# Chunk attention and two MoE layers on one core: exponentials head by head with the maximum as bias, and another order of the first loads

## The chip, the cores and the metric

The kernel runs on one core of a Trainium2 chip. Five engines work side by side, each through its own queue in program order: TensorE (PE, matrix products, with the weight loads listed as PEld), VectorE (DVE), ScalarE (ACT), GpSimd (POOL) and SyncE (SP, which here issues the DMA transfers). The metric is the device time of one execution in microseconds (us); lower is better. Time before the change: 1680.23 us, the median of three runs (1678.89 to 1683.86).

## What is computed

```python
scores = scale * np.matmul(q_c, k_c.transpose(0, 1, 2, 4, 3))   # chunks of 64 tokens, 8 heads, 64 wide
scores = scores - np.max(scores, axis=-1, keepdims=True)
attn = np.exp(scores)
attn = attn / (np.sum(attn, axis=-1, keepdims=True) + 1e-09)
x = np.matmul(attn, v_c)                                        # laid out as 4608 tokens x 512
h = x @ w_in1                                                   # 512 -> 2048
x = (np.maximum(h, 0) + alpha * np.minimum(h, 0)) @ w_out1      # 2048 -> 512
h = x @ w_in2
out = (h - np.tanh(h)) @ w_out2
```

The weights and alpha arrive as 64-bit numbers and are turned into 32-bit ones on the chip; q, k and v are 32-bit.

## The kernel before

The 4608 tokens are cut into 36 tiles of 128 and into 9 blocks of 512 (four tiles). Every float32 product of the two layers is made from three products of rounded halves ("hi" and "lo"), which the code calls `split`. The program is written out by hand in its final order: what stands first in the source stands first in the queue of its engine.

**The opening** handles tiles 0 to 3 and ends when block 0 can be multiplied. For each tile: `att_a_early` transposes q and k on PE (into `tr`) and copies the result out (`qt`, `kt`, line 290 on DVE or 292 on ACT); `att_s_early` makes the scores with 32 small matmuls (line 335); `att_e` takes the maximum of each head over the 64 scores (`mx`, DVE, line 348), subtracts it (`p`, DVE, line 350) and takes the exponential of all eight heads in one instruction (ACT, line 353); `att_n` sums (DVE, line 359), adds 1e-9 (361), takes the reciprocal (362) and multiplies (363, on POOL for tiles 0 to 2); `att_t_early` transposes `p` on PE (`ptr`, line 403) and copies it out on ACT (405); `att_v_early` multiplies by v (418); `att_x` splits the result into xh (ACT, 435) and xl (DVE, 439). The scores of tiles 0 to 3 go in turn to the two halves of one tile `first_banks`, two PSUM banks that are called `first` in the trace.

**Weights.** The first piece is "s0", the second "s1", then pairs 0, 1, 2 and so on. `load_w` issues the transfer, `convert_a` makes two ACT passes (lines 113 and 116, or 113 and 162), `convert_b` four DVE passes that the code numbers as ops 0 to 3 (lines 126, 130, 132, 136), and `split_w` a rounded copy on ACT (174) and a difference (181). The buffer `wr` that `convert_low` (162) writes exists once, so it waits for op 3 of the piece before.

**The step loop.** A step multiplies one block by one of the 16 column pieces of w_in1 (`up`, line 455, 12 matmuls), applies the activation (`act_g`, lines 467 to 469) and, two steps later, multiplies by w_out1 (`down`, line 511). Steps 0 to 7 run `step_first`: beside its own work each pair of steps takes one tile of block 1 (tiles 4 to 7) through attention and converts two more weight pairs. In an even step the order on DVE is: op 0, `att_e`, ops 1 and 2, `att_n`, the splits, op 3, the activation. The copy of the next tile's `kt` (292) then stands on ACT behind line 162, and the next step's `up` needs the PSUM buffer that this copy frees. Steps from 16 on (`step_one`, `step_two`) and tiles from 8 on keep their code.

**Loads.** SP issues everything in the order of the `load_...` calls; every transfer is on one queue.

Of the kernel before, what the change touches and what calls it, by code (L numbers as in the profile page):

```python
# [27 lines left out]
def kernel(  # L28
# [111 lines left out]
    def load_w(d):  # L140
        raw_w[d] = home(d, [P, len(PAIRS[d]), 512], I64, "raww")
        for i, (f, which) in enumerate(PAIRS[d]):
            load_raw(raw_w[d][:, i], 0, f, which)
# [21 lines left out]
    def convert_b(d, ops=(0, 1, 2, 3)):  # L165
        to_f32_b([w_parts[d]], ops)
# [174 lines left out]
                    )  # L341
        scs[t] = sc

    def att_e(t, early=False):
        scv = scs.pop(t)
        a, b = (HP, 2) if early else (2, HP)
        mx = stat.tile([P, a, b, 1], F32, tag="mx", name="mx")
        nc.vector.tensor_reduce(out=mx[:, :, :, 0], in_=scv, op=ALU.max, axis=AX.X)
        p = first_p[:, t] if t < NPT else att.tile([P, H, D], F32, tag="p", name="p")
        nc.vector.tensor_tensor(  # L350
            out=p.rearrange("p (a b) d -> p a b d", a=a), in0=scv, in1=mx.to_broadcast([P, a, b, D]), op=ALU.subtract
        )
        nc.scalar.activation(out=p, in_=p, func=AF.Exp, scale=scale)
        ps[t] = p

    def att_n(t, engine=nc.vector):
        p = ps[t]
        sm = stat.tile([P, H], F32, tag="sm", name="sm")
        nc.vector.tensor_reduce(out=sm, in_=p, op=ALU.add, axis=AX.X)
        rd = stat.tile([P, H, 1], F32, tag="rd", name="rd")  # L360
        nc.vector.tensor_scalar(out=sm, in0=sm, scalar1=1e-9, scalar2=None, op0=ALU.add)
        nc.vector.reciprocal(out=rd[:, :, 0], in_=sm)
        engine.tensor_tensor(out=p, in0=p, in1=rd.to_broadcast([P, H, D]), op=ALU.mult)
# [303 lines left out]
    def load_first(t):  # L667
        load_natural(t, first_raw[t // 2][:, t % 2])
# [6 lines left out]
    load_first(3)  # L675
    load_v(0)
    load_v(1)
    load_w("s1")
    load_v(2, first_v[:, 0])
    load_v(3, first_v[:, 1])  # L680
    arow = stage.tile([P, 512], F32, tag="st", name="arow")
    nc.sync.dma_start(out=arow[:KF, :P], in_=alpha.rearrange("(f p) -> f p", p=P))
    load_first(4)
    load_w(0)
    load_w(1)
    load_first(5)
    load_v(4, first_v[:, 2])
# [19 lines left out]
    att_a_early(1, 0)  # L707
    att_s_early(0)
    att_a_early(1, 1)
    att_e(0, True)  # L710
    warm(3)
    att_s_early(1)
    att_n(0, nc.gpsimd)
    convert_a("s0")
    att_a_early(2, 0)
    att_e(1, True)
    warm(4)
    att_a_early(2, 1)
    convert_b("s0", ops=(0, 1))
# [4 lines left out]
    convert_b("s0", ops=(2,))  # L724
    att_a_early(3, 0)
    att_a_early(3, 1)
    att_e(2, True)
    convert_b("s0", ops=(3,))
    warm(3)
    att_s_early(3)  # L730
# [2 lines left out]
    split_w("s0", nc.gpsimd)  # L733
    warm(1)
    att_v_early(0)
    att_e(3, True)
    att_t_early(2)
    att_xh(0, x0, 0)
    att_v_early(1)
    convert_a("s1")  # L740
    att_n(3)
    att_xl(0, x0, 0)
    more = first_banks[:, 0, 0:P]
# [4 lines left out]
    att_xl(1, x0, P)  # L748
    hp0 = up(0, x0, NB, slice(0, 2 * P))
    att_xh(2, x0, 2 * P)  # L750
    convert_b("s1", ops=(0, 1))
    att_xl(2, x0, 2 * P)
    att_v_early(3)
    at_ps = first_banks[:, 0, 0:KF]
    nc.tensor.transpose(at_ps, arow[:KF, :P], ident[:KF, :KF])
    new_first(NPT)
    att_xh(3, x0, 3 * P)
    convert_b("s1", ops=(2, 3))
    att_xl(3, x0, 3 * P)
    split_w("s1", nc.vector)  # L760
    att_a_second(4)
    nc.scalar.activation(out=nalpha_sb, in_=at_ps, func=AF.Copy, scale=-1.0)
    convert_a(0)
    load_v(6)
# [20 lines left out]
    def step_first(step, j, t0, f, ends, x, acc):  # L785

        d, t, even = step, NPT + step // 2, step % 2 == 0
        now, more, last = d < HF - 1, d + 1 < HF - 1, 0 < d  # L790

        def some(ops):
            if now:
                convert_b(d, ops)

        def lows(order):
            for what in order:
                if what == "w" and last:
                    split_w_lo(d - 1, nc.vector)
                if what == "g" and late:  # L800
                    split_lo(*late.pop(), nc.vector)

        if even and step:
            att_s_early(t)
        if late:
            split_hi(*late[0])
        if not even:
            att_t_early(t)
        if last:
            split_w_hi(d - 1)  # L810
        some((0,))
        if step == 0:
            hp = up(f, x, NB, slice(2 * P, NB), hp0)
            att_s_early(t)
        if even:
            att_e(t, True)
        some((1, 2))
        if step:
            hp = up(f, x, NB)
        if even:  # L820
            att_n(t)
            lows("wg")
        else:
            lows("gw")
        some((3,))
        g = act_g(0, f, hp, NB)
        queue.append((0, f, g, acc, j, t0, ends))
        late.append(g)
        if step == 1:
            att_a_second(t + 1)  # L830
        elif even and step and t + 1 < 2 * NPT:
            att_a_early(t + 1, 0)
        if not even:
            att_v_early(t)
            att_x(t, get_x(1), t % NPT * P)
        if more:
            convert_high(d + 1)
            convert_low(d + 1)
        if len(queue) == LAG + 1:
            next_down()  # L840
        if even and step and t + 1 < 2 * NPT:
            att_a_early(t + 1, 1)
        fire(step)
# [75 lines left out]
```

## Time and profile before

| | |
|---|---|
| median of three runs | 1680.23 us |
| the profiled execution, its own time | 1681.05 us |
| its span in the trace | 1679.2 us (1.85 us lie around it) |
| PE busy | 1651.2 us, 98% |
| DVE busy | 1291.5 us, 77% |
| ACT busy | 817.0 us, 49% |
| POOL busy | 231.7 us, 14% |
| DMA | 112.77 MB, mean 67 GB/s |

Busy shares are means over stages with different limits. A row of a timeline gives start and duration in us, engine, source line, operation, what is written and read, how many instructions were merged, and in square brackets how long the engine had stood idle before and what released it. The rows used below stand in their own section.

### The profile page before, as it was taken

How to read it: one execution, taken by the hardware profiler on the slowest of the kernel's cores; microseconds unless marked ns; L12 is line 12 of the kernel's file. 1: busy time of each engine (PE TensorE's matmuls, PEld its weight loads, DVE VectorE, ACT ScalarE, POOL GpSimd, SP SyncE). 2: the span in 40 equal slices, each digit the busy share in tenths (PEclk: the TensorE clock that was granted, in tenths of full speed). 3: DMA queues.
4: the chain of work that ended last, by engine and by line, in shares of the span. 5: the costliest groups of instructions: out<-in, count | busy, mean ns of one | idle time of the engine just before them, and what ended most of it. 6: DMA issues, size and time to landing. Idle time of an engine off the chain costs nothing.

```text
span 1679.2 us, 24428 instructions
## 1 busy us (share of the span) xinstructions
PE 1651.2 (98%) x9405; PEld 1360.4 (81%) x9405; DVE 1291.5 (77%) x1864; ACT 817.0 (49%) x1465; POOL 231.7 (14%) x171
## 2 busy tenths in 40 slices
PE   7899999999999999999999999999999999999998
PEld 6688888888887888888887888888888888888886
DVE  7878855666666666564358989898989998999987
ACT  5756544454544454454445444444444444444443
POOL 1000000000000000000146222222222222222221
PEclk9999999999999999999999999999999999999999
DMA  9661424333333333431333010101010101010000
GB/s 228 192 188 40 114 52 100 95 95 86 90 84 102 87 90 70 101 95 39 113 100 114 1 51 1 51 0 51 0 51 1 51 1 51 1 41 10 20 7 26
DMA packets 215269, 112.77 MB, mean 67 GB/s; under 512 B 170592, under 2 KB 186992, under 8 KB 215152
## 3 DMA queue, kind: packets, MB, share of 16 engines
q1 hardware_dynamic: 215152, 111.20, 24.1%
q8 instruction: 74, 1.21, 0.3%
q14 instruction: 43, 0.35, 0.1%
HBM read 81.80 MB, written 29.36 MB: 66 GB/s over the span
## 4 chain that ended last, share of the span: by engine, by line
PE 92%; DVE 3%; SPq 2%; DMA 1%; issue 1%; ACT 1%; DVEq 0%; ACTq 0%
PE y L511 45%; PE hps L455 45%; PE sc L318 1%; SPq L224 1%; DVE g L501 1%; SPq L219 1%; PE sc L389 1%; DVE g L500 0%; DMA ysc<-yst 0%; DMA first<-in_k_dram 0%; SPq L99 0%; DVE g L498 0%; DVE wm L132 0%; PE tr L276 0%; DVE wm L136 0%
## 5 line engine op out<-in xcount | busy, mean ns | idle before, releaser
L455 PE MATMUL hps<-xh,w 128*128 128x512 f32 (+1 forms) x2312 | 573.3, 390 | 5.2 <-ACT kt L292 5.2
L455 PEld LDWEIGHTS hps<-xh,w 128*128 128x128 f32 x2312 | 434.2, 188 | 95.7 <-ACT kt L292 5.7
L455 PE MATMUL hps<-xl,w 128*128 128x512 f32 (+1 forms) x1156 | 309.0, 389 | 0.0
L511 PE MATMUL y<-ghi,w 128*128 128x512 f32 x1152 | 300.6, 394 | 2.7 <-ACT yst L531 2.7
L511 PE MATMUL y<-w,ghi 128*128 128x512 f32 x1152 | 293.9, 390 | 2.5 <-ACT ghi L481 2.5
L493 ACT ACTIVATE sq<-hps 128x512 f32<-128x512 f32 x144 | 86.1, 598 | 401.0 <-PE hps L455 400.5
L484 POOL TENSOR_TENSOR glo<-g,ghi 128x512 fp32r<-128x512 f32 x144 | 185.6, 1289 | 579.9 <-ACT ghi L481 579.9
L511 PEld LDWEIGHTS y<-w,ghi 128*128 128x128 f32 x1152 | 215.8, 188 | 49.0 <-ACT ghi L481 4.4
L455 PEld LDWEIGHTS hps<-xl,w 128*128 128x128 f32 x1156 | 217.5, 188 | 45.2
L511 PEld LDWEIGHTS y<-ghi,w 128*128 128x128 f32 x1152 | 213.1, 188 | 48.4 <-ACT yst L531 3.2
L469 DVE SCALAR_TENSOR_TENSOR g<-neg,nalpha_sb,g 128x512 f32<-128x512 f32 x144 | 107.4, 746 | 179.3 <-ACT g L468 179.3
L500 DVE SCALAR_TENSOR_TENSOR g<-w,g 128x512 f32<-128x512 f32 x144 | 243.4, 1690 | 0.0
L481 ACT ACTIVATE ghi<-g 128x512 fp32r<-128x512 f32 x288 | 181.5, 630 | 103.9 <-DVE g L469 86.1
L467 ACT ACTIVATE neg<-hps 128x512 f32<-128x512 f32 x144 | 85.9, 597 | 222.4 <-PE hps L455 220.9
L511 PE MATMUL y<-glo,w 128*128 128x512 f32 x576 | 164.7, 389 | 0.0
L511 PE MATMUL y<-w,glo 128*128 128x512 f32 x576 | 162.8, 389 | 0.0
L181 POOL TENSOR_TENSOR w<-wm,w 128x1024 fp32r<-128x1024 f32 (+1 forms) x18 | 42.2, 2346 | 840.5 <-ACT w L174 840.5
L484 DVE TENSOR_TENSOR glo<-g,ghi 128x512 fp32r<-128x512 f32 x144 | 108.2, 751 | 33.7 <-ACT ghi L481 32.9
L511 PEld LDWEIGHTS y<-w,glo 128*128 128x128 f32 x576 | 108.1, 188 | 22.9 <-DVE glo L484 0.4
L511 PEld LDWEIGHTS y<-glo,w 128*128 128x128 f32 x576 | 108.1, 188 | 22.4
L501 DVE SCALAR_TENSOR_TENSOR g<-sq,g 128x512 f32<-128x512 f32 x144 | 110.1, 764 | 5.0
L502 DVE COPY_PREDICATED g<-ktc,th 128x512 f32<-128x512 uint32 x144 | 108.5, 753 | 4.9
(95 smaller groups left out, 1384.0 us busy)
## 6 DMA issues: line engine op xcount, KB each, us to landing
yraw<-ysc SPq DMA_DIRECT2D x9, 1024.0 KB, 5.8
out_dram<-yst SPq DMA_DIRECT2D x36, 256.0 KB, 2.2
raww<-in_moe_w_in_dram SPq DMA_DIRECT2D x16, 512.0 KB, 6.3
v<-in_v_dram SPq DMA_DIRECT2D x32, 256.0 KB, 4.2
raww<-in_moe_w_out_dram SPq DMA_DIRECT2D x16, 512.0 KB, 6.0
rw<-in_moe_w_in_dram SPq DMA_DIRECT2D x16, 512.0 KB, 4.3
w<-mr SPq DMA_DIRECT2D x32, 256.0 KB, 2.1
rw<-in_moe_w_out_dram SPq DMA_DIRECT2D x16, 512.0 KB, 4.1
```

The lines of the kernel that those rows point to most:

```text
L181: lo_engine.tensor_tensor(out=w_[:, :, 1], in0=w, in1=w_[:, :, 0].bitcast(F32), op=ALU.subtract)
L219: nc.sync.dma_start(out=vt[off:off + n], in_=v[b, :, s:s + n, :].rearrange("h p d -> p h d"))
L455: nc.tensor.matmul(out=hp[:, cols], lhsT=w[:, a, m], rhs=x[b][:, kk, cols], start=(kk == 0 and i == 0), stop=(kk == KD - 1 and i == 2),)
L467: nc.scalar.activation(out=neg, in_=hp, func=AF.Relu, scale=-1.0)
L469: nc.vector.scalar_tensor_tensor(out=g, in0=neg, scalar=nalpha_sb[:, f:f + 1], in1=g, op0=ALU.mult, op1=ALU.add)
L481: nc.scalar.activation(out=hi, in_=g, func=AF.Copy)
L484: lo_engine.tensor_tensor(out=lo, in0=g, in1=hi.bitcast(F32), op=ALU.subtract)
L493: nc.scalar.activation(out=sq, in_=hp, func=AF.Square)
L500: nc.vector.scalar_tensor_tensor(out=g, in0=w, scalar=ce, in1=g, op0=ALU.add, op1=ALU.mult)
L501: nc.vector.scalar_tensor_tensor(out=g, in0=sq, scalar=ca, in1=g, op0=ALU.add, op1=ALU.mult)
L502: nc.vector.copy_predicated(g, mask, th)
L511: nc.tensor.matmul(out=acc[t], lhsT=lhsT, rhs=rhs, start=(f == ends[0] and i == 0), stop=(f == ends[1] and i == 2))
```

## The change

For tiles 0 to 7 `att_e` is replaced by `att_e_early`. It takes the maximum on DVE as before, multiplies the 128x8 result by minus the scale (a new small DVE instruction), and then issues eight ACT instructions per tile, one for each head: each reads 64 scores from PSUM, adds the scaled maximum as a bias held in memory, takes the exponential, writes 64 columns of `p`, and gives the sum over these 64 columns as a second output. The subtraction (line 350) and the sum (line 359) are gone for these tiles; `att_n` takes the sums as they are. Tiles from 8 on keep the old form.

Of the order: the loads of v for tiles 2 and 3 go ahead of "s1", and that of weight pair 0 ahead of q and k of tile 4. `convert_a("s1")` moves from behind `att_v_early(1)` to behind `att_v_early(3)`, with ops 0 and 1 right behind it; `att_xl(3)` goes ahead of ops 2 and 3. The transposes of tile 4 move from the end of the opening into step 0, behind the second half of its `up`. In step 0 ops 1, 2 and 3 of pair 0 go ahead of the exponentials (before: 1 and 2 behind them, 3 behind `att_n`).

```diff
@@ -341,22 +341,39 @@
                     )
         scs[t] = sc
 
-    def att_e(t, early=False):
+    sums = {}
+
+    def att_e(t):
         scv = scs.pop(t)
-        a, b = (HP, 2) if early else (2, HP)
-        mx = stat.tile([P, a, b, 1], F32, tag="mx", name="mx")
+        mx = stat.tile([P, 2, HP, 1], F32, tag="mx", name="mx")
         nc.vector.tensor_reduce(out=mx[:, :, :, 0], in_=scv, op=ALU.max, axis=AX.X)
-        p = first_p[:, t] if t < NPT else att.tile([P, H, D], F32, tag="p", name="p")
+        p = att.tile([P, H, D], F32, tag="p", name="p")
         nc.vector.tensor_tensor(
-            out=p.rearrange("p (a b) d -> p a b d", a=a), in0=scv, in1=mx.to_broadcast([P, a, b, D]), op=ALU.subtract
+            out=p.rearrange("p (a b) d -> p a b d", a=2), in0=scv, in1=mx.to_broadcast([P, 2, HP, D]), op=ALU.subtract
         )
         nc.scalar.activation(out=p, in_=p, func=AF.Exp, scale=scale)
         ps[t] = p
 
+    def att_e_early(t):
+
+        scv = scs.pop(t).rearrange("p h c d -> p (h c) d")
+        mx = stat.tile([P, H], F32, tag="mx", name="mx")
+        nc.vector.tensor_reduce(out=mx, in_=scv, op=ALU.max, axis=AX.X)
+        nc.vector.tensor_scalar(out=mx, in0=mx, scalar1=-scale, scalar2=None, op0=ALU.mult)
+        ps[t] = p = first_p[:, t] if t < NPT else att.tile([P, H, D], F32, tag="p", name="p")
+        sums[t] = stat.tile([P, H], F32, tag="sm", name="sm")
+        for h in range(H):
+            nc.scalar.activation(
+                out=p[:, h, :], in_=scv[:, h, :], func=AF.Exp, scale=scale, bias=mx[:, h:h + 1],
+                accum_out=sums[t][:, h:h + 1],
+            )
+
     def att_n(t, engine=nc.vector):
         p = ps[t]
-        sm = stat.tile([P, H], F32, tag="sm", name="sm")
-        nc.vector.tensor_reduce(out=sm, in_=p, op=ALU.add, axis=AX.X)
+        sm = sums.pop(t, None)
+        if sm is None:
+            sm = stat.tile([P, H], F32, tag="sm", name="sm")
+            nc.vector.tensor_reduce(out=sm, in_=p, op=ALU.add, axis=AX.X)
         rd = stat.tile([P, H, 1], F32, tag="rd", name="rd")
         nc.vector.tensor_scalar(out=sm, in0=sm, scalar1=1e-9, scalar2=None, op0=ALU.add)
         nc.vector.reciprocal(out=rd[:, :, 0], in_=sm)
@@ -675,13 +692,13 @@
     load_first(3)
     load_v(0)
     load_v(1)
-    load_w("s1")
     load_v(2, first_v[:, 0])
     load_v(3, first_v[:, 1])
+    load_w("s1")
     arow = stage.tile([P, 512], F32, tag="st", name="arow")
     nc.sync.dma_start(out=arow[:KF, :P], in_=alpha.rearrange("(f p) -> f p", p=P))
+    load_w(0)
     load_first(4)
-    load_w(0)
     load_w(1)
     load_first(5)
     load_v(4, first_v[:, 2])
@@ -707,13 +724,13 @@
     att_a_early(1, 0)
     att_s_early(0)
     att_a_early(1, 1)
-    att_e(0, True)
+    att_e_early(0)
     warm(3)
     att_s_early(1)
     att_n(0, nc.gpsimd)
     convert_a("s0")
     att_a_early(2, 0)
-    att_e(1, True)
+    att_e_early(1)
     warm(4)
     att_a_early(2, 1)
     convert_b("s0", ops=(0, 1))
@@ -724,7 +741,7 @@
     convert_b("s0", ops=(2,))
     att_a_early(3, 0)
     att_a_early(3, 1)
-    att_e(2, True)
+    att_e_early(2)
     convert_b("s0", ops=(3,))
     warm(3)
     att_s_early(3)
@@ -733,11 +750,10 @@
     split_w("s0", nc.gpsimd)
     warm(1)
     att_v_early(0)
-    att_e(3, True)
+    att_e_early(3)
     att_t_early(2)
     att_xh(0, x0, 0)
     att_v_early(1)
-    convert_a("s1")
     att_n(3)
     att_xl(0, x0, 0)
     more = first_banks[:, 0, 0:P]
@@ -748,17 +764,17 @@
     att_xl(1, x0, P)
     hp0 = up(0, x0, NB, slice(0, 2 * P))
     att_xh(2, x0, 2 * P)
-    convert_b("s1", ops=(0, 1))
     att_xl(2, x0, 2 * P)
     att_v_early(3)
+    convert_a("s1")
+    convert_b("s1", ops=(0, 1))
     at_ps = first_banks[:, 0, 0:KF]
     nc.tensor.transpose(at_ps, arow[:KF, :P], ident[:KF, :KF])
     new_first(NPT)
     att_xh(3, x0, 3 * P)
+    att_xl(3, x0, 3 * P)
     convert_b("s1", ops=(2, 3))
-    att_xl(3, x0, 3 * P)
     split_w("s1", nc.vector)
-    att_a_second(4)
     nc.scalar.activation(out=nalpha_sb, in_=at_ps, func=AF.Copy, scale=-1.0)
     convert_a(0)
     load_v(6)
@@ -811,10 +827,13 @@
         some((0,))
         if step == 0:
             hp = up(f, x, NB, slice(2 * P, NB), hp0)
+            att_a_second(t)
             att_s_early(t)
+            some((1, 2, 3))
         if even:
-            att_e(t, True)
-        some((1, 2))
+            att_e_early(t)
+        if step:
+            some((1, 2))
         if step:
             hp = up(f, x, NB)
         if even:
@@ -822,7 +841,8 @@
             lows("wg")
         else:
             lows("gw")
-        some((3,))
+        if step:
+            some((3,))
         g = act_g(0, f, hp, NB)
         queue.append((0, f, g, acc, j, t0, ends))
         late.append(g)
```

## Rows read from the trace of the kernel before

**Rows 1.** Busy time by stage (us, instruction counts in brackets, granted clock, DMA share, GB/s).

```profile
30.00:40.00 10.00, 4.26 (x42) 3.66 (x43) 8.66 (x14) 6.74 (x10) 0.00 (x0) 0.77 1.03 249
50.00:60.00 10.00, 7.41 (x39) 5.78 (x37) 9.83 (x14) 6.33 (x9) 0.00 (x0) 1.00 1.11 280
100.00:110.00 10.00, 10.00 (x50) 8.38 (x49) 6.17 (x8) 7.10 (x11) 0.00 (x0) 1.00 0.34 110
```

**Rows 2.** Waits from 0 to 100 us: total, times, longest.

```profile
PE first L335 <- DVE p L350: 1.2, 2, 0.9
```

**Rows 3.** Timeline of the opening, tiles 0 and 1.

```profile
8.36 0.69 DVE L348 TENSOR_REDUCE mx<-first 128x8 f32<-128x512 f32 x1 [1.66 <-PE first L335]
...
8.93 0.60 ACT L292 ACTIVATE kt<-tr 128x512 f32<-128x512 f32 x1 [1.07 <-PE tr L287]
9.08 0.69 DVE L350 TENSOR_TENSOR p<-first,mx 128x512 f32<-128x512 f32 x1
...
9.92 1.15 PE L335 MATMUL first<-kt,qt 64*64 64x64 f32 x32 [0.36 <-DVE p L350]
...
14.96 1.09 PE L287 MATMUL tr<-ident,first 128*128 128x128 f32 x8
```

**Rows 4.** Timeline: the last exponential of the opening, then step 0.

```profile
20.65 0.63 ACT L353 ACTIVATE p<-p 128x512 f32<-128x512 f32 x1 [0.18 <-DVE p L350]
...
31.09 0.69 DVE L126 TENSOR_SCALAR wm<-wm 128x1024 f32<-128x1024 f32 x1 [1.38 <-ACT wm L113]
...
36.89 1.08 PE L403 MATMUL ptr<-ident,p 128*128 128x128 f32 x4 [5.66 <-DVE p L363]
```

**Rows 5.** Groups by line and form, 30 to 100 us: busy, mean ns, idle before.

```profile
L132 DVE SCALAR_TENSOR_TENSOR wm<-raww,wm 128x1024 int32<-128x1024 int32 x7 | 8.6, 1225 | 0.2
...
L350 DVE TENSOR_TENSOR p<-sc,mx 128x512 f32<-128x512 f32 x4 | 2.8, 691 | 0.1
...
L359 DVE TENSOR_REDUCE sm<-p 128x8 f32<-128x512 f32 x4 | 2.7, 678 | 0.0
...
L353 ACT ACTIVATE p<-p 128x512 f32<-128x512 f32 x4 | 2.5, 632 | 3.0 <-DVE p L350 3.0
...
L362 DVE RECIPROCAL rd<-sm 128x8 f32<-128x8 f32 x4 | 0.8, 203 | 0.1
L361 DVE TENSOR_SCALAR sm<-sm 128x8 f32<-128x8 f32 x4 | 0.7, 172 | 0.1
```

**Rows 6.** Groups of ACT by form, whole span.

```profile
L481 ACT ACTIVATE ghi<-g 128x512 fp32r<-128x512 f32 x288 | 181.5, 630 | 103.9 <-DVE g L469 86.1 <-DVE g L502 17.9
L495 ACT ACTIVATE w<-sq,bias_sb 128x512 f32<-128x512 f32 x144 | 104.3, 724 | 0.0
...
L468 ACT ACTIVATE g<-hps 128x512 f32<-128x512 f32 x144 | 85.5, 594 | 0.0
...
L762 ACT ACTIVATE nalpha_sb<-first 128x16 f32<-128x16 f32 x1 | 0.2, 186 | 0.0
```

**Rows 7.** Timeline of ACT in the second layer, instructions that follow each other at once.

```profile
1203.56 0.72 ACT L495 ACTIVATE w<-sq,bias_sb 128x512 f32<-128x512 f32 x1
1204.18 0.63 ACT L481 ACTIVATE ghi<-g 128x512 fp32r<-128x512 f32 x1
```

**Rows 8.** Timeline of one pair of steps (4 and 5), to the next.

```profile
64.86 0.69 DVE L348 TENSOR_REDUCE mx<-sc 128x8 f32<-128x512 f32 x1 [1.27 <-PE sc L335]
...
72.81 1.15 ACT L162 ACTIVATE wr<-raww 128x1024 int32<-128x1024 uint32 x1 [0.53 <-DVE wm L136]
...
74.49 2.12 PE L455 MATMUL hps<-xh,w 128*128 128x512 f32 x8 [2.64 <-ACT kt L292]
...
82.21 0.69 DVE L348 TENSOR_REDUCE mx<-sc 128x8 f32<-128x512 f32 x1 [1.28 <-PE sc L335]
```

**Rows 9.** DMA issues from 0 to 100 us: count, KB each, median us to landing.

```profile
raww<-in_moe_w_in_dram SPq DMA_DIRECT2D x15, 512.0 KB, 6.3
...
first<-in_q_dram SPq DMA_DIRECT2D x7, 256.0 KB, 6.4
```

## The prediction

> **What bounds the kernel now.** The page alone misleads here: PE is busy for 98% of the span, so one looks for matmuls to remove, and the change removes none. I read the busy time by stage first. From 100 us on PE has no free moment [rows 1]; what follows is a fixed row of matmuls, and the end of the kernel moves by just as much as the start of that stretch. Before it the picture is another one: from 30 to 40 us PE works 4.26 of 10 us and DVE 8.66, from 50 to 60 PE 7.41 and DVE 9.83 [rows 1]. So the change is worth what it does to the first 100 us, and nothing in them is absorbed later. The second view is the waits, for the opening: PE twice waits for line 350, the subtraction [rows 2]. The third is the timeline of a pair of steps, for the loop: the pair's period is 82.21 - 64.86 = 17.35 us, and its ring runs through DVE from the maximum to op 3, which releases ACT's L162 at 72.81, then through the copy of kt to PE at 74.49, and through up, the product with v, down and the scores back to the maximum [rows 8].
>
> **The price of one tile's exponentials, X.** Removed per tile: a subtraction of 0.691, a sum of 0.678 and one exponential of 0.632; added: a multiplication of 128x8, for which I take the 0.172 of L361, and eight ACT instructions [rows 5]. DVE thus saves 1.20 us a tile, 9.6 us in all eight. No row shows an ACT instruction with 64 columns, a bias and a second output, so I bound it. From 16 to 512 columns a plain one goes from 186 to 594 ns [rows 6], 0.82 ns a column. With a bias from memory 512 columns take 724 against 630 ns [rows 6], 94 more. What counts in a row of eight is the distance of their starts: L495, with its bias, is followed after 1204.18 - 1203.56 = 0.62 us [rows 7]; less 448 columns of 0.82 ns that leaves 0.25 us. Lower bound: the second output is free, X = 8 x 0.25 + 0.09 for the tail of the last = 2.05 us. Upper bound: each needs an instruction of its own as long as the smallest row, 0.186 [rows 6], so X = 3.5. I take 2.8, half way: the nearest row is for an instruction that stores 16 columns, and the sums store one, half overlapped as instructions in the rows are. If the engine must finish each exponential before its sum can be read, X is about 4.0; that is a rival. X below 2.05 would need a start distance shorter than the bias rows show.
>
> On the same price the Trainium skill ("ScalarE: Activation LUTs", section "What ACT_TABLE_LOAD costs") says that an ACTIVATE with a [128,1] bias takes about 280 ns plus 0.833 ns a column and that neighbours overlap by 93 ns. By that page X would be 8 x 0.24 + 0.09 = 2.0 us and the whole sum 6.4 us in place of the 12.2 below. It speaks against the change all the same, since the fixed part is paid eight times, and names no price for the accumulator output. Its 707 ns for 512 columns stands beside the trace's 724 [rows 6].
>
> **The opening.** This is the step on which the forecast hangs. PE starts the scores of tile 1 at 9.92, after 0.36 us of waiting for the subtraction of tile 0, which ends at 9.08 + 0.69 = 9.77 [rows 3]; kt was ready at 9.53 [rows 3]. The scores of tiles 0 and 1 lie in different banks, but both banks are one tile, `first_banks`, and the wait is for the last reader of that tile. The new last reader is the eighth exponential. So the ring per tile becomes: maximum 0.69, multiplication 0.17, X, scores 1.15, and about 0.25 for the hand-overs, 2.26 + X us, with nothing overlapping it. In tiles 1 to 3 ACT has in front of the exponentials copies of 0.60 [rows 3] of transposes that PE does only after the scores (0.55 for four, 1.09 for eight [rows 3]): a copy of qt for tile 1, of kt for tile 2, of ptr and the rounding of s0 for tile 3. Beyond the 0.95 us in which DVE gets the bias ready they cost some 0.3, 0.75 and 0.85 us. The scores of tile 0 end at about 8.31, 0.05 before the maximum [rows 3]; 0.95 for the bias, 0.15 for the kt copy in front on ACT, 1.9 of such extras, three rings: the last exponential of tile 3 ends at 8.31 + 0.95 + 0.15 + 1.9 + 6.8 + 4X = 18.1 + 4X. Before it ends at 20.65 + 0.63 = 21.28 [rows 4]. Difference 4X - 3.2: **+5.0, +8.0 or +10.8 us** for X = 2.05, 2.8 and 3.5.
>
> **The end of the opening and step 0.** Ops 0 and 1 of s1, until now done in a gap of DVE, go between xl(2) and xl(3): two passes of half of the 0.69 of L126's width [rows 4], some 0.8 us with the hand-over. From op 0 of pair 0 (31.09) to the transposes of tile 4 (36.89) it takes 5.80 us now [rows 4]. New: op 0 and 1 at 0.69 [rows 4] and op 2 and 3 at 1.22 [rows 5] make 3.9 with gaps, then the maximum and its multiplication 0.86, X, 1e-9, reciprocal and multiplication 0.17 + 0.20 + 0.69 = 1.06 [rows 5] and 0.3 of hand-overs: 6.1 + X. The scores of tile 4 come later than before, since its transposes do and its copies stand behind the two ACT passes of pair 0, but still before op 3 ends, so they cost nothing; were they late, the 1.15 us of the scores would show. Moving op 3 ahead gains nothing after the transposes: there up(1) is PE's own work. Sum 0.8 + 6.1 + X - 5.8 = 1.1 + X: **+3.2, +3.9 or +4.6 us**.
>
> **The three pairs of steps 2 to 7.** On DVE from the maximum to the end of op 3 now: 72.81 - 64.86, 7.95 with the hand-over [rows 8]. New: 0.95 to the first exponential, X (ops 1 and 2, 1.9 us, lie beside it), 1.06 + 0.1 for the rest of `att_n`, then the two splits and op 3, 3.1 with widths as in L132 and L350 [rows 5]: 5.25 + X. Per pair -0.65, +0.1 or +0.8; of the last pair PE can give back little. Over three: **-1.7, +0.3 or +2.4 us**. The sign turns at X = 2.7: the 1.20 us that DVE saves come back as waiting for ACT.
>
> **The loads.** A transfer lands 6.3 or 6.4 us after its issue [rows 9], so the order decides, not SP. s1 goes some 2 us later and q and k of tile 4 some 4 us (1 MB in front of them at the 249 GB/s of [rows 1]). I cost both at nothing, because the opening that uses them ends 8 us later; without that cover tile 4's transposes would wait up to 4 us. The loads brought forward release nobody: no PE wait in the opening names them.
>
> **Sum.** +6.5 (X = 2.05), **+12.2** (2.8), +17.8 (3.5), on the profiled execution's 1681.05 us: 1693.3. Its span is 1679.2 and 1.85 lie around it. It lies 0.8 above the median of 1680.23; put on the median the forecast is **1692.4 us**, from 1686.7 to 1698.0.
>
> **The rivals.** *The banks are independent* (0.14). The scores of tile t+1 don't wait for ACT, so only ACT's own queue counts in the opening: there the four exponentials go from 0.63 each to X and partly fill ACT's idle time, which leaves about +0.5 (X = 2.05) to +3.2 (2.8) in place of 5.0 to 8.0. With the other two parts +2.0 to +7.4: 1682.2 to 1687.6, in the middle 1685. For it: the two halves are separate banks. Against it: the wait of [rows 2] is for such another bank, twice.
>
> *DVE's relief decides: faster* (0.12). In the steps, where DVE works 9.83 of 10 us [rows 1], the exponentials end before op 2 if 0.95 + X is under 0.95 + 1.9, which needs X of 1.9 or less, 0.23 us for each; then a pair loses 0.8 and three 2.4. In the opening tiles 1 to 3 give back 1.2 each, 3.6. That is 6.0 together: 1674.2. It needs the banks to be independent and X under my lower bound, and no clock to lose; the bias rows speak against it, the busy share of DVE for it. A part of it, PE not falling to the lower clock before step 1 (0.77 of full in [rows 1]), would give some 2 us.
>
> *Each sum waits for its exponential* (0.08): X = 4.0, opening +12.8, step 0 +5.1, pairs +3.9: 1702.0.
>
> **How the numbers follow.** My forecast has 0.66; its bounds are 1686.7 and 1698.0. The measurement can tell about 0.3%, 5 us, from no change. Forecast and last rival are slower by more than that, less a little at the lower edge; of the independent banks a third is slower, the rest within; the faster rival is faster by more than 5 us in most of its cases. Slower 0.74, same 0.16, faster 0.10. For 8 in 10 the range leaves out the faster rival and the last one, and takes in the independent banks: 1682.2 to 1698.0.
>
> **What would show it.** In the trace after: the scores of tile 1 start at 9.92 (independent banks) or at 11.5 to 13 behind an ACT exponential (forecast); the start distance of the exponentials, 0.25 to 0.43 us, fixes X; the last exponential of tile 3 ends at 26 to 32; the transposes of tile 4 start at 45 to 52 in place of 36.89; the pairs' period, 17.35, changes by less than 1 us; PE's free stretch begins 6 to 18 us later. The forecast is wrong if the wait names something else than ACT, or if PE runs up(1) at its full clock after all.

## The result, and the profile after

The kernel after takes 1689.85 us in the median of four runs (1688.80 to 1691.63), beside 1679.7 us for the kernel before (1678.89 to 1683.86): ratio 1.0057, 95% interval 1.0037 to 1.0076. That is slower by 0.57%, inside the range, 2.5 us below the forecast of 1692.4. The profiled execution took 1690.44 us with a span of 1688.3.

On the page almost nothing has moved: PE is still busy for 98%, DVE works 8 us less (1283.3 in place of 1291.5) and ACT 14 us more (830.9 in place of 817.0). Busy time and the clock of the page of after:

```profile
PE 1655.9 (98%) x9405; PEld 1365.5 (81%) x9405; DVE 1283.3 (76%) x1856; ACT 830.9 (49%) x1585; POOL 232.5 (14%) x171
...
PEclk8899999999999999999999999999999999999999
```

Busy time by stage of after, to be laid beside [rows 1] (columns as there):

```profile
30.00:40.00 10.00, 7.90 (x101) 7.10 (x101) 5.73 (x14) 5.07 (x13) 0.00 (x0) 0.83 0.98 232
50.00:60.00 10.00, 7.91 (x86) 6.37 (x85) 7.52 (x11) 7.55 (x14) 0.00 (x0) 0.77 1.15 312
100.00:110.00 10.00, 9.45 (x71) 7.53 (x70) 5.91 (x9) 4.64 (x9) 0.00 (x0) 1.00 0.73 254
```

From 100 to 110 us PE is no longer without a gap: the stretch that was in its free run in the kernel before [rows 1] is still in the pairs of steps. DVE's share from 30 to 40 has fallen from 8.66 to 5.73, and the program is no earlier for it. The waits of after from 0 to 100 us (total, times, longest) say what DVE and PE now wait for:

```profile
DVE sm L378 <- ACT p L366: 13.9, 7, 3.7
...
PE ptr L420 <- DVE p L380: 4.8, 1, 4.8
PE first L335 <- ACT p L366: 4.8, 2, 2.4
...
PE sc L335 <- ACT kt L292: 3.1, 1, 3.1
```

In the place of PE's two waits of 0.9 us at most for the subtraction on DVE [rows 2] stand two of 2.4 us for the exponentials on ACT. DVE waits 13.9 us for the sums, seven times. In the kernel before, the first instruction that needs the exponentials on DVE was the sum, and it waited 1.4 us in all:

```profile
DVE sm L359 <- ACT p L353: 1.4, 2, 0.7
```

The timeline of after, with the landmarks that answer to [rows 3, 4, 8]:

```profile
9.12 0.60 ACT L292 ACTIVATE kt<-tr 128x512 f32<-128x512 f32 x1 [1.08 <-PE tr L287]
9.27 0.17 DVE L362 TENSOR_SCALAR mx<-mx 128x8 f32<-128x8 f32 x1
...
9.62 0.31 ACT L366 ACTIVATE p<-first,mx 128x64 f32<-128x64 f32 x1
9.81 0.20 ACT L366 ACTIVATION_READ_ACCUMULATOR p<-first,mx 128x1 f32 x1
9.91 0.31 ACT L366 ACTIVATE p<-first,mx 128x64 f32<-128x64 f32 x1
...
11.83 0.25 ACT L366 ACTIVATION_READ_ACCUMULATOR p<-first,mx 128x1 f32 x1
...
12.14 1.15 PE L335 MATMUL first<-kt,qt 64*64 64x64 f32 x32 [2.38 <-ACT p L366]
...
17.66 1.15 PE L335 MATMUL first<-kt,qt 64*64 64x64 f32 x32
...
22.94 1.22 PE L335 MATMUL first<-kt,qt 64*64 64x64 f32 x32 [2.43 <-ACT p L366]
...
28.46 0.25 ACT L366 ACTIVATION_READ_ACCUMULATOR p<-first,mx 128x1 f32 x1
...
39.90 0.69 DVE L126 TENSOR_SCALAR wm<-wm 128x1024 f32<-128x1024 f32 x1 [0.39 <-ACT wm L113]
...
48.72 1.09 PE L420 MATMUL ptr<-ident,p 128*128 128x128 f32 x4 [4.82 <-DVE p L380]
49.45 3.76 PE L472 MATMUL hps<-xh,w 128*128 128x512 f32 x8
...
76.86 0.69 DVE L361 TENSOR_REDUCE mx<-sc 128x8 f32<-128x512 f32 x1 [1.27 <-PE sc L335]
...
93.80 0.69 DVE L361 TENSOR_REDUCE mx<-sc 128x8 f32<-128x512 f32 x1 [1.28 <-PE sc L335]
```

Read as distances, before against after:

| stretch | before | after | difference |
|---|---|---|---|
| start to the end of tile 3's last exponential | 21.28 | 28.71 | +7.4 |
| from there to op 0 of pair 0 | 9.81 | 11.19 | +1.4 |
| from there to the transposes of tile 4 | 5.80 | 8.82 | +3.0 |
| from there to the maximum of tile 5 | 10.62 | 10.89 | +0.3 |
| maximum of tile 5 to tile 6, tile 6 to tile 7 | 17.35, 17.35 | 17.25, 16.94 | -0.1, -0.4 |
| from there to the activation of step 7, where PE's free run (no more waits until 530 us) begins | 10.57 | 10.16 | -0.4 |
| sum at that point | | | +11.2 |

The span is longer by 9.1, not 11.2. The missing 2.1 us lie at one place, 440 us later, that the change doesn't touch: the first `down` after PE has waited for `yst`, ACT's copy of a finished block out of PSUM. There the kernel before shows

```profile
532.44 0.74 PE L511 MATMUL y<-ghi,w 128*128 128x512 f32 x2 [2.74 <-ACT yst L531]
...
533.26 3.25 PE L455 MATMUL hps<-xh,w 128*128 128x512 f32 x8
```

and the kernel after

```profile
543.10 0.74 PE L528 MATMUL y<-ghi,w 128*128 128x512 f32 x2 [2.22 <-ACT yst L548]
...
543.92 2.01 PE L472 MATMUL hps<-xh,w 128*128 128x512 f32 x8
```

The same eight matmuls take 3.25 us in one profile, where the granted clock is 0.87 and 0.79 from 530 to 540, and 2.01 in the other, where it is 1.00; the four behind them take 1.46 and 1.07. With 0.5 us less of waiting that makes the 2.1 us. Of the fourteen profiles of this case three show the low clock at this place (before, runs 3 and 7) and eleven don't. All three have the old order (three of seven, beside none of seven with the new one); whether the order has a part in it, one profile for each kernel doesn't settle.

### The profile page after: what moved, and what is told of

The parts are those of the page before. It is cut to its first block, busy times and chain, and to the rows that moved or that the text cites. A ratio compares the mean times of both kernels' runs of the same rounds, so it can differ in the third digit from the quotient of the medians.

```text
span 1688.3 us, 24546 instructions
## 1 busy us (share of the span) xinstructions
PE 1655.9 (98%) x9405; PEld 1365.5 (81%) x9405; DVE 1283.3 (76%) x1856; ACT 830.9 (49%) x1585; POOL 232.5 (14%) x171
## 4 chain that ended last, share of the span: by engine, by line
PE 91%; DVE 3%; ACT 1%; issue 1%; DMA 1%; SPq 0%; ACTq 0%; DVEq 0%
PE y L528 45%; PE hps L472 44%; PE sc L318 1%; DVE g L518 1%; PE sc L406 1%; DVE g L517 0%; DMA ysc<-yst 0%; ACT p L366 0%; DVE g L515 0%; PE tr L276 0%; DVE wm L136 0%; DVE w L181 0%; ACT ghi L498 0%; DVE g L519 0%; ACT wr L162 0%
```

## The experiments

The change has three parts (exponentials, their sums, order), and most runs put in or take out one of them. Two theories were on trial. **The forecast**: the new wait of the scores for ACT, through the one tile `first_banks`, carries the loss. **Its rivals**: ACT's own queue carries it, whatever the banks; or the changed order does. Each ratio is to the kernel before on the same chip, whose medians lie between 1679.05 and 1681.09 us.

**1. The wait taken away: two tiles for the two banks.** Tiles 0 to 3 write their scores into two tiles of one bank each, so that the scores of tile t+1 wait for no reader of tile t.

```diff
-    first_banks = new_banks("first")
+    first_banks = [ps_f.tile([P, 512], F32, tag=f"f{i}", name=f"first{i}") for i in range(2)]
-        bank = first_banks[:, t % 2] if t < NPT else new_banks("sc")[:, 0]
+        bank = first_banks[t % 2] if t < NPT else new_banks("sc")[:, 0]
```

> The changed kernel, but the two PSUM banks for the scores of tiles 0 to 3 are two tiles, so that the scores of tile t+1 need not wait for the last exponential of tile t. Theory 1 (the wait for the shared tile makes most of the loss in the opening): the scores of tile 1 start near 10 us in place of 12.14, the last exponential of tile 3 ends near 23 us in place of 28.7, and the time falls by 4 to 6 us from the changed kernel's 1689.9, to about 1684.5. Rival 2 (ScalarE's own queue is full: 8 x 0.29 us a tile whatever waits): the last exponential of tile 3 still ends after 27 us and the time stays within 2 us of 1689.9. Rival 3 (the new order costs the time, not the exponentials): no change, 1689.9.

Measured: 1686.74 us, ratio 1.0045 (1.0032 to 1.0058). The timeline of this kernel:

```profile
9.37 0.31 ACT L371 ACTIVATE p<-first,mx 128x64 f32<-128x64 f32 x1
9.52 1.01 PEld L340 LDWEIGHTS first<-kt,qt 64*64 64x64 f32 x32 [0.21 <-ACT kt L297]
9.52 1.15 PE L340 MATMUL first<-kt,qt 64*64 64x64 f32 x32
...
24.56 0.24 ACT L371 ACTIVATION_READ_ACCUMULATOR p<-first,mx 128x1 f32 x1
```

The scores of tile 1 start at 9.52, beside the exponentials of tile 0 and released by the copy of kt: the wait is gone, so it was the shared tile. But the last exponential of tile 3 still ends at 24.80, where before has 21.28. The wait is the smaller part of the loss in the opening. The larger part comes from X as well, by another way: the maximum of tile 1, in DVE's order behind `att_n` of tile 0, starts at 12.19, after the sums (11.87) that wait for the eighth exponential. That is read from the timeline; no run changed this order on DVE. The time fell by 0.12% (2.0 us), less than the 4 to 6 us expected, and the intervals of the two kernels overlap, so it is the trace that shows the wait gone, not the time.

**2. The order alone**, with the exponentials of the kernel before in all tiles:

```diff
-        for h in range(H):
-            nc.scalar.activation(
-                out=p[:, h, :], in_=scv[:, h, :], func=AF.Exp, scale=scale, bias=mx[:, h:h + 1],
-                accum_out=sums[t][:, h:h + 1],
-            )
+        nc.vector.tensor_tensor(
+            out=p.rearrange("p (a b) d -> p a b d", a=HP), in0=scv, in1=mx.to_broadcast([P, HP, 2, D]), op=ALU.subtract
+        )
+        nc.scalar.activation(out=p, in_=p, func=AF.Exp, scale=scale)
```

> The changed kernel's order of loads and of work, with the old subtraction, single exponential and sum for all tiles. Theory 1: the opening is back near 21.3 us for the last exponential of tile 3; what is left is the order's part, 0.8 us for s1 and some 2.2 us in step 0 (its three passes of pair 0 now stand ahead of the exponential): 1683, 3 us above before. Rival 2: within 1 us of before. Rival 3: the whole loss, 1689 to 1690.

**3. The exponentials alone**, in the order of the kernel before, loads included (the same edit the other way, made in `att_e` and `att_n` of the kernel before).

> The exponentials head by head for tiles 0 to 7 with the order of before everywhere (loads, s1, step 0). Theory 1: the opening loses its 7.4 us, step 0 gains 0.4 since ops 1 and 2 lie beside the exponentials, the pairs gain 0.5: 1686 to 1687. Rival 2: the same, 1686 to 1688. Rival 3: 1680, as before.

**4. The new order with the new exponentials in tiles 4 to 7 only**; tiles 0 to 3 subtract on DVE as before, in `att_e_sub`.

```diff
     def att_e_early(t):
+        if t < NPT:
+            return att_e_sub(t)
```

> The changed kernel, but tiles 0 to 3 keep the subtraction and the single exponential; tiles 4 to 7 go head by head. Theory 1: the opening's 7.4 us are back; left are 0.8 for s1, 3.5 for step 0 (its exponentials of 2.5 us stand behind all passes of pair 0) and a gain of 0.5 in the pairs: 1683.5. Rival 2: the same within 1 us. Rival 3: 1689 to 1690.

Measured: order alone 1683.46, ratio 1.0019 (1.0011 to 1.0028); exponentials alone 1685.23, 1.0032 (1.0021 to 1.0042); new exponentials from tile 4 on 1682.82, 1.0016 (1.0007 to 1.0025). The two parts add up: 0.19% and 0.32% make 0.51%, and both together measure 0.57%. In the traces each loses where it should: with the order alone the last exponential ends at 21.44 as before, and op 0 to the transposes of tile 4 takes 40.10 - 31.94 = 8.16 us; with the exponentials alone that end is 27.27, and the same stretch 41.72 - 36.34 = 5.38. The loss of run 4 lies in that stretch too (40.59 - 31.86 = 8.73). The rows of runs 2 and 3:

```profile
31.94 0.69 DVE L126 TENSOR_SCALAR wm<-wm 128x1024 f32<-128x1024 f32 x1 [0.39 <-ACT wm L113]
...
40.10 1.09 PE L417 MATMUL ptr<-ident,p 128*128 128x128 f32 x4 [4.16 <-DVE p L377]
```

```profile
36.34 0.69 DVE L126 TENSOR_SCALAR wm<-wm 128x1024 f32<-128x1024 f32 x1 [1.37 <-ACT wm L113]
...
41.72 0.66 PE L420 MATMUL ptr<-ident,p 128*128 128x128 f32 x2 [5.23 <-DVE p L380]
```

In run 2 DVE works almost without a gap from op 0 to the maximum at 35.99. So 2.4 of the +3.0 us of step 0 belong to ops 1 to 3 ahead of the exponentials, with the old exponentials already. The new ones add 0.7 in this order (8.82) and take 0.4 away in the old one (5.38). From the last exponential to op 0, a stretch that the prediction counts by itself, run 2 takes 10.50 us, run 4 10.50, run 3 9.07 and before 9.81: the order costs 0.7 there and the new exponentials give 0.7 back. The stretches also explain the times: the order loses 0.7 + 2.4 = 3.1 us (0.19% is 3.2), the exponentials 6.0 - 0.7 - 0.4 = 4.9 us up to the transposes of tile 4 (0.32% is 5.4).

**5. The sums back on DVE.** The exponentials keep their bias, `accum_out` is left out, and `att_n` sums again:

```diff
-                accum_out=sums[t][:, h:h + 1],
```

> The changed kernel, but the exponentials give no sums; DVE sums again (0.68 us a tile). Theory 1: the reads of the accumulator, one between any two exponentials, are the part of the 0.29 us that is not in the bias row, so the exponentials follow each other at 0.20 to 0.25 us, each tile's eight take 1.7 to 2.1 in place of 2.45, the rings of the opening shorten by 0.4 to 0.75 each, and the time is 1687 to 1689. Rival: an exponential with a bias keeps the distance of 0.29 without the second output; then the sums on DVE come on top, 1690 to 1692.

Measured: 1688.33, ratio 1.0043 (1.0029 to 1.0056). One row of its timeline holds all eight exponentials of tile 0:

```profile
9.37 1.74 ACT L365 ACTIVATE p<-first,mx 128x64 f32<-128x64 f32 x8
```

Without the second output they start (1.74 - 0.31) / 7 = 0.20 us apart, with it 0.29 (9.62 and 9.91 above). Of X = 2.46 us, 0.72 is the price of the sums, against the 0.68 that DVE saves: in this kernel moving the sums to ACT is no saving even as busy time. The run also tries the weight of X in the opening. The last exponential of tile 3 ends at 24.63, against 27.28 in the kernel after at full clock (the profile after_warm of run 8): 2.65 us for 0.72 us of X in each of four tiles, where the prediction's 4X would give 2.9. The time doesn't tell this run from after, as the intervals overlap: from there to op 0 it takes 11.83 us, with the sum of tile 3 back on DVE and a granted clock of 0.86 and 0.80 from 25 to 35 us.

**6. The loads of before.** The kernel after with the load order of the kernel before, nothing else.

```diff
+    load_w("s1")
     load_v(2, first_v[:, 0])
...
-    load_w("s1")
...
-    load_w(0)
     load_first(4)
+    load_w(0)
```

> The changed kernel with the order of loads of before. Theory 1 (loads are hidden on both sides): landmarks within 0.3 us of the changed kernel, 1689.9. Rival: the new order of loads is late for tile 4, then this one is 1 to 4 us faster; or it is what brings pair 0 in time, then this one is 1 to 4 us slower.

Measured: 1689.01, ratio 1.0052 (1.0037 to 1.0068), beside 1.0057. Nothing that can be told from none. The landmarks are not within the 0.3 us expected: op 0 comes at 38.13, 1.8 us before that of after. But the clock differs too: from 30 to 35 us it is 1.00 here and 0.66 in the profile of after, and after_warm, at full clock, has op 0 at 37.07. Behind that stands this run by 1.1 us, with a granted clock of 0.70 from 10 to 15 us, where its scores of tile 1 take 1.90 us in place of 1.15. PE's waits for transfers come to 0.4 us in the first 30. So the loads cost and give nothing that shows.

**7. The part that should pay.** If DVE's relief is worth anything, it is in the pairs of steps, so the kernel before gets the new exponentials in tiles 5, 6 and 7 alone, its own order kept.

```diff
     def att_e_early(t):
+        if t <= NPT:
+            return att_e_sub(t)
```

> The kernel before with the exponentials head by head for tiles 5 to 7 alone, old order everywhere. Theory 1: the pairs of steps take 0.1 to 0.4 us less each, as they do in the changed kernel's trace (17.25 and 16.94 us against 17.35), some 0.9 together: 1679. Rival (only the wait for ScalarE is moved): no change or slower by up to 1 us.

Measured: 1679.39, ratio 0.9993 (0.9984 to 1.0002): no change that can be told. One of its two full pairs takes 17.0 us and the other 18.5, with a granted clock of 0.88 and 0.78 from 70 to 80 us, inside the second.

**8. The lower clock in step 1, before and after.** The prediction named up(1), which PE runs at half rate in both kernels. Dummy matmuls behind the scores of tile 4 keep PE at work through its wait; in the kernel after there are 18 in place of 20, in the kernel before 9 more in steps 3 and 5 each:

```diff
             att_s_early(t)
+            warm(20, ps_y.tile([P, P], F32, tag="y0", name="wt"))
```

> The kernel before, with 20 matmuls of zeros behind the scores of tile 4, in PE's idle time of step 0, and 9 in steps 3 and 5 between the transposes and up, where PE waits for kt. Nothing else is changed. Theory 4 (PE falls to its lower clock after such idle times and then runs the next matmuls at half rate): up in step 1 takes 3 in place of 5.1 us, 2 us less in all, 1677.5. Rival: the clock falls all the same, or the zeros delay the transposes of tile 4: 1680 or above.

> The kernel after with 18 dummy matmuls behind the scores of tile 4 in step 0, so that PE does not stand still for 4.8 us before the transposes of tile 4; nothing else changes. In the profile of after the scores of tile 4 take 1.97 us and up(1) 3.76 + 1.82 us at a granted clock of 0.50 to 0.54, where full clock would give 1.2 and 2.1 + 1.07. Theory (part of the new wait's cost is PE's lower clock behind it): up(1) takes about 3.1 us in place of 5.6, the maximum of tile 5 comes 1 to 2.5 us earlier than 59.61, time 1687.5 to 1689 beside 1689.9 for after. Rival (DVE's queue or the copies of step 1 are the bound behind up(1), as in the same edit on the kernel before): up(1) is shorter but the maximum of tile 5 comes within 0.5 us of 59.6, time 1689.9.

Measured: on the kernel before 1679.12, ratio 0.9990 (0.9982 to 0.9999); on the kernel after 1687.04, ratio 1.0035 (1.0023 to 1.0048). PE in the kernel before with dummies:

```profile
37.54 2.09 PE L459 MATMUL hps<-xh,w 128*128 128x512 f32 x8
...
45.81 1.98 PE L339 MATMUL sc<-kt,qt 64*64 64x64 f32 x32 [3.77 <-DVE xl L443]
47.71 3.78 PE L459 MATMUL hps<-xh,w 128*128 128x512 f32 x8
```

and in the kernel after with dummies:

```profile
40.98 6.26 PE L714 MATMUL wt<-zero 128*128 128x128 f32 x36
...
47.43 2.10 PE L472 MATMUL hps<-xh,w 128*128 128x512 f32 x8
...
54.03 1.15 PE L335 MATMUL sc<-kt,qt 64*64 64x64 f32 x32 [2.09 <-DVE xl L456]
```

In both, up(1) runs at full rate (2.1 us for eight matmuls, in place of 3.76 in after), and PE then stands still before the scores of tile 5, for DVE's xl. In the kernel before this wait, 2.09 us without dummies, grows to 3.77 and takes the whole gain: the maximum of tile 5 comes at 47.82 (47.51 without dummies). The half rate has only moved on, to the scores (1.98 in place of 1.15) and the next up (3.78). In the kernel after the wait stays at 2.09, as without dummies. There it is the dummies that take a part: they end at 47.24, and the transposes of tile 4 start 10.00 us after op 0 in place of 8.82. From op 0 to the maximum of tile 5 it is 18.15 us in place of 19.71, a gain of 1.6. The rest of its lead of 4.4 us at that point, 2.8 us, is older than the edit, and the last section takes it up. By time, the intervals of after with and without dummies overlap.

The eleven executions of the kernel before with dummies lie closer together than those without: 1678.23 to 1679.60 us, beside 1678.06 to 1684.29 for the twenty-one of the kernel before on the same chip. Their mean granted clock is 0.997 to 0.999, that of the others 0.994 to 0.998. The best execution is no better; what the median gains comes from the slow executions that are missing.

**9. Do the separate banks pay elsewhere?** The split of run 1 in the kernel with the exponentials alone (run 3), and in the kernel of run 7.

> The kernel before with the head-by-head exponentials in tiles 0 to 7, its own order of everything else, and first_banks split into two tiles of one bank each. Exponentials alone cost 5.3 us (1685.2 beside 1679.9). If the parts add up, the split gives back what it gave in the kernel after, about 3 us: 1682 (last exponential of tile 3 at 23 to 25 in place of 27.3). If the order of the loads and passes is what lets the split pay, it gives back under 1 us: 1684.5 or more. If the exponentials on separate banks were the gain that the change was after, it is under 1679.

> The kernel before with the head-by-head exponentials in tiles 5, 6 and 7 alone (which by themselves gave 1679.4 beside 1680.0) and first_banks split into two tiles. The split frees the scores of tile 1 from the wait of 0.36 us and of tile 2 from 0.9 us, the two waits of the kernel before on the subtraction. Theory (the opening is a ring through that wait): the last exponential of tile 3 ends 0.5 to 1.2 us before 21.2, time 1678 to 1679. Rival (maximum and subtraction on DVE follow each other anyway): 1679.4, within 0.3 us.

Measured: 1683.06, ratio 1.0016 (1.0007 to 1.0025), where run 3 had 1.0032: it gives back 2.7 us, beside 2.0 in run 1, which these intervals don't tell apart, and the last exponential of tile 3 ends at 24.88 in place of 27.27. So the split pays in either order. In the kernel of run 7: 1679.33, ratio 0.9990 (0.9981 to 0.9999), where run 7 had 0.9993. There the last exponential of tile 3 ends at 21.04, 0.24 us earlier than before: the rival was right, and the waits of [rows 2] had cost the kernel before next to nothing. The maximum of tile 1 comes 3.16 us after that of tile 0 with one tile and with two.

**10. All that had helped, in one kernel**: runs 7, 8 and 9 together on the kernel before.

> The three edits of the kernel before that by themselves gave 0.7 to 1.8 us together: head-by-head exponentials in tiles 5, 6 and 7 alone, first_banks as two tiles, and dummy matmuls in step 0 (20 behind the scores of tile 4) and in steps 3 and 5 (9 each) that keep PE from standing still. If what each gave is a gain of its own, they add to 2 to 3.5 us: ratio 0.9980 to 0.9988, time 1677 to 1678.5 beside 1680. If it is the same gain each time, namely that the opening's queue on DVE sets the end and the clock's dips fall here or there, the ratio stays at 0.9990 to 0.9995.

Measured: 1677.87, ratio 0.9991 (0.9982 to 1.0000). By the ratio the gains don't add up, but the interval takes in what both theories forecast, so the run doesn't decide between them. The four kernels of runs 7 to 10 that start from before lie at 0.9990 to 0.9993, alone or together: at most 0.2% faster, and none can be told from another.

## Why the prediction was right, point by point

**The bound and the window.** This was right: the end moves with the start of PE's free run, and nothing between 100 and 530 us absorbs any of it.

**X.** The step's interval was 2.05 to 3.5 with 2.8 taken; measured 12.08 - 9.62 = 2.46 us, one exponential every 0.29. The second output is an instruction of its own, as the upper bound supposed, with a row of 0.20 us, of which some 0.09 show in the distance of the starts. The other end was too high as well: without it the distance is 0.20, and not the 0.25 taken from the rows with 512 columns. An estimate from the figures of the Trainium skill ("ScalarE: Activation LUTs", section "What ACT_TABLE_LOAD costs") is 0.24 for that; the run shows 0.20. With the X of 2.0 that the prediction worked out from the Trainium skill (the same section), the whole sum is about 6.1 and not the 6.4 that it wrote. The lower bound of the step, 8 x 0.25 + 0.09, is 2.09 and not 2.05. Neither touches the forecast.

**The opening.** Predicted +8.0, and +6.6 for an X of 2.46; measured +7.4. The ring (a chain in which each instruction waits for the one before, and which starts again with the next tile) was described rightly: scores of tile 1 at 12.14 behind ACT's exponential (11.5 to 13 was forecast), end at 28.71 (26 to 32). The extras on ACT were 14.50 - 14.23 = 0.3, 0.5 and 1.2 us for tiles 1, 2 and 3, where 0.3, 0.75 and 0.85 stood. What the step didn't have is that PE runs part of this at its lower clock in this profile: after_warm, whose program is the same up to there, ends the last exponential at 27.28, which is +6.0, and so does run 3 in the old order (27.27). So at full clock the step was 0.6 too high. There PE waits for the exponentials in all three rings; in the profile of after it does so in two, and the scores of tile 2 (17.66) start behind the copy of their kt. Where the step argued too simply is the weight of its mechanism. Of those 6.0 us only 2.4 to 2.5 go when the banks are independent (24.80 and 24.88 in runs 1 and 9); some 3.5 stay; by the timeline of run 1 DVE's order closes a second ring there, over the same X. The rival with independent banks put this remainder at 0.5 to 3.2, on a straight line between its two values about 2.0 for the X measured. It was wrong about the wait and too low on what is left without it.

**The end of the opening.** Predicted +0.8 for the passes of s1 between xl(2) and xl(3). In the profile of after it is +1.4, but three profiles of the same order and exponentials in which the clock of this stretch is full (runs 1 and 6, and after_warm) need 9.77, 9.77 and 9.79 us from the last exponential to op 0, as before (9.81). The term was right all the same. The order costs 0.7 with either exponentials: 9.81 becomes 10.50 (run 2), and 9.07 (run 3) becomes 9.77, all at a granted clock of 1.00. What the step left out is that the new exponentials shorten this stretch by 0.7, since the sum of tile 3 on DVE is gone from it. The first row is from before, the second from after_warm, each the first of DVE behind the last exponential:

```profile
21.32 0.69 DVE L359 TENSOR_REDUCE sm<-p 128x8 f32<-128x512 f32 x1 [0.70 <-ACT p L353]
...
27.31 0.17 DVE L378 TENSOR_SCALAR sm<-sm 128x8 f32<-128x8 f32 x1 [3.20 <-ACT p L366]
```

The two make nothing together. In the profile of after the granted clock is 0.77 from 25 to 30 us and 0.66 from 30 to 35, and that goes with the 1.4.

**Step 0.** Predicted 6.1 + X - 5.8, which is +2.8 at the X measured; measured +3.0. This is the best step of the sum. Run 2 shows that the order makes the most of it: with the old exponentials the stretch is 8.16 in place of 5.80.

**The pairs.** Predicted between -0.65 and +0.8 each, by the step's sum -0.24 for the X measured; measured -0.1 and -0.4. DVE waits 0.74 us for the sums after op 2, and the ring through ops and splits is as predicted. So DVE's relief of 1.20 us in each of these tiles, 3.6 in all, gives 0.9 us from the maximum of tile 5 to the free run.

**The loads.** Predicted nothing; measured nothing that can be told from it (run 6).

**Sum.** The steps with the X measured give 6.6 + 0.8 + 2.8 - 0.7 = 9.5 us; the medians differ by 10.2, the ratio says 9.6. That the forecast of 12.2 came out 2.5 us high is X: 0.34 us too much, eight times (four in the opening, once in step 0, three in the pairs), is 2.7 us. In the two profiles the clock adds to this on both sides: that of after has lost 2.8 us up to op 0 against after_warm (0.2 of it before the first maximum, where the clock is full in both), that of before 2.1 us at 533 us. That 9.5 comes so close to 9.6 is therefore partly luck. At full clock the opening and its end are 6.6 + 0.8 by the steps and 6.0 + 0.0 in the traces, and the four executions of after ran at a mean granted clock of 0.992 to 0.995, those of before at 0.994 to 0.998.

**The landmarks.** All came inside what was written: distance 0.29 (0.25 to 0.43), transposes of tile 4 at 48.72 (45 to 52), pairs within 1 us of 17.35, free run 11.2 us later (6 to 18), the wait on ACT, up(1) at half rate.

**The faster rival** fell by its own conditions: X is 2.46, and it needed 1.9 and independent banks. Even the exponentials without sums (1.74) don't save it, since their sum of 0.68 then goes back to DVE.

**The spread between executions** goes with the clock. Each of the 82 executions of the kernel before that stand beside the runs has its mean granted clock on record: the nine with the lowest, 0.994, took 1682.2 to 1684.3 us, the 34 at 0.996 1679.3 to 1682.0, and the 25 with the highest, 0.998, 1678.1 to 1679.5. What makes the clock fall in one execution and not in the next is not shown.

## What to carry to other kernels

Relieving the busiest engine of a stretch pays only where that engine's next instruction doesn't then wait for the engine that takes the work over: DVE had 8 us less to do and waited 13.9 us for the sums, where it had waited 1.4 for the exponentials. A fused instruction with a per-partition bias and a sum has to be priced per issue and not per element; cut into eight, a 0.63 us exponential became 2.46 us. When a consumer moves to another engine, look at who reads the buffer last: two banks declared as one tile let the slower reader of one bank hold up the writer of the other, and two tiles gave back 2.4 to 2.5 of the 6.0 us that the opening had lost at full clock. When two edits meet in one stretch, run each alone: the passes of s1 seemed free in the kernel after, and cost 0.7 us that the missing sum paid for.

## What the runs showed of the hardware

**The sum as second output is a second instruction.** Each such ACTIVATE is followed by an ACTIVATION_READ_ACCUMULATOR with a row of 0.19 to 0.31 us that overlaps its neighbours; it widens the distance of the starts from 0.20 to 0.29 us.

**After the same wait PE sometimes runs on at half rate and sometimes not.** The plainest place is the one wait for `yst` near 530 us, since PE has had no other wait for over 400 us there. In run 7 PE waits 2.40 us and then runs at half rate for a while (granted clock 0.74 and 0.58 from 530 to 532.5 and from 532.5 to 535), in run 4 it waits 2.67 us and runs on at full rate:

```profile
531.57 1.22 PE L541 MATMUL y<-ghi,w 128*128 128x512 f32 x2 [2.40 <-ACT yst L561]
...
533.02 2.74 PE L485 MATMUL hps<-xh,w 128*128 128x512 f32 x8
```

```profile
534.86 0.73 PE L541 MATMUL y<-ghi,w 128*128 128x512 f32 x2 [2.67 <-ACT yst L561]
...
535.66 1.99 PE L485 MATMUL hps<-xh,w 128*128 128x512 f32 x8
```

After waits of 2.50 (run 3) and 2.74 us (before) the clock fell too, after 2.22 (after), 2.27 (the second kernel of run 9), 2.65 (run 5) and 2.69 (run 1) it didn't. So the length of the wait alone doesn't decide it.

The opening shows the same between two executions. Up to step 0 the kernels after and after_warm are the same program, and PE waits some 2.4 us for the exponentials in both. Clock by stretches of 5 us in the profile of after:

```profile
10.00:15.00 5.00, 2.86 (x42) 2.80 (x43) 1.24 (x4) 4.20 (x22) 1.04 (x1) 0.86 1.13 209
15.00:20.00 5.00, 5.00 (x59) 4.81 (x58) 3.32 (x9) 3.13 (x17) 1.31 (x1) 0.79 0.98 225
...
30.00:35.00 5.00, 4.66 (x59) 4.26 (x63) 2.42 (x7) 2.42 (x7) 0.00 (x0) 0.66 0.86 185
```

and in that of after_warm:

```profile
10.00:15.00 5.00, 3.06 (x50) 2.99 (x51) 1.24 (x4) 4.30 (x23) 1.04 (x1) 1.00 1.32 219
15.00:20.00 5.00, 3.74 (x55) 3.29 (x52) 3.84 (x9) 3.66 (x19) 1.32 (x1) 1.00 0.94 194
...
30.00:35.00 5.00, 4.31 (x62) 4.00 (x62) 3.39 (x8) 2.83 (x7) 0.00 (x0) 1.00 1.01 202
```

Op 0 of pair 0 comes at 39.90 in the one and at 37.07 in the other: 2.8 us between two executions of the same instructions. Inside one stretch the clock goes between its two levels of 1.2 and 2.4 GHz, and 0.66 to 0.86 are means. The same is seen in the pairs: in run 2 PE waits 2.65 us, in [rows 8] 2.64, and then needs

```profile
59.79 2.63 PE L469 MATMUL hps<-xh,w 128*128 128x512 f32 x8 [2.65 <-ACT kt L292]
62.22 1.91 PE L469 MATMUL hps<-xl,w 128*128 128x512 f32 x4
```

where [rows 8] have 2.12 for the first row, and the pair takes 18.9 us in place of 17.35. So a difference of 1.3 to 2.8 us between two single profiles of this kernel may be nothing but that, and edits worth 1 us, as those of runs 7 to 10, need the medians of many executions.
